# A longer hand-written order of exponentials, projections and V products in the first attention block of a transformer layer

## The chip, the cores and the metric

The kernel runs on one core of one Trainium2 chip. The metric is device time in microseconds (us), the median of the timed runs. A core has five engines that run their own instruction streams and wait for each other through semaphores: PE (TensorE, matrix products), ACT (ScalarE, here the exponentials), DVE (VectorE), POOL (GpSimd) and SP (which issues DMAs here).

## What is computed

A pre-norm transformer layer for 2048 tokens of width 512: attention with 32 query heads of width 16 that share one key head and one value head, then a gated feed-forward network of width 1792, both with a residual.

```python
h  = x + softmax(heads(ln(x) @ wq) @ (ln(x) @ wk).T * 16 ** -0.5) @ (ln(x) @ wv) @ wo
h2 = h + (gelu(ln(h) @ w_gate) * (ln(h) @ w_up)) @ w_down
```

All inputs are float32. Most products are made of split operands, a high and a low part, in three terms.

## The kernel before, in words

**Blocks, groups, exponentials.** The 2048 queries are four blocks of 512. A block has eight groups of four heads (`NG`), and a group has 16 chunks of 128 keys (`KC`). One chunk of one group is a *pair* of exponentials. One exponential is one tile `s` of 128 keys x 2 heads x 512 queries: two score matmuls on PE (L460, `s<-qg,kaug`) into PSUM, then one ACT instruction (L464, `p<-s`) that reads the tile and writes half of a tile `p`. So a group has 32 exponentials and a block 256. They are counted by `n`; group k of the first block holds n = 32(k-1) to 32k-1. In the first block there are three tiles `s` (two of one pool, one more while `width` is 1) and five tiles `p` (`PB`).

**V products.** When both exponentials of a pair are done, the pair can be multiplied with V: function `weigh` (L468, `acc<-p,v_sb`), four matmuls side by side in column strips of 32, which the profile shows as 8 records. This is called a *run*. The 16 runs of a group add up in one PSUM bank, `acc`, of which there is one. After run 15 `evacuate` copies the bank to SBUF on DVE (L481, `oT<-acc`), and its result goes through a DRAM buffer (`acc_d`, `oc`) to be divided by the softmax sums (reciprocals, L509, and two or three more DVE steps), in small steps that are taken out of a list, `outs`, one per run. Run 0 of the next group writes the same bank. Pairs that wait for their run stand in the list `pend`; `finish(n)` does the n oldest.

**The projection beside it.** In the first block PE also projects the queries of blocks 2 to 4 (`project_q`, L458, `pq<-xT,wq`): 12 blocks of work of two halves, each half 12 half-height matmuls ("tokens"), 288 tokens in all. A half-height product uses 64 of the 128 rows of PE, a score uses 50, so that a product and a score run side by side. An exponential of kind "m" (mixed) takes two tokens with it; one of kind "s" takes none. When a half ends inside a step, the rest of that step's "m" are done as "s". After each half DVE makes a mark (L243), after each block a copy (L258), then a split into high and low (L143, L144) and squares (`qs`), which feed a norm on PE (L294, `pqn`). While a norm is due, a step is done without products.

**The order.** A loop (`while n < lead`) writes out the first block. Each turn is a *step*: a word of kinds such as "mms", then a number of runs. PE, ACT, POOL, and in this block DVE and SP too, execute in just that order. Before the change the step is found by `r % 10`, with r = n mod 32: `MIXED = {0: ("mms", 2), 3: ("smm", 1), 6: ("mm", 1), 8: ("ss", 1)}`, and for r of 30 and 31 "sm" or "mm" with one run. The word is made lighter or heavier by comparing the tokens that are left with the exponentials up to `LAST_Q` = 258. A step does its runs only if more than two pairs wait. At 7 places of a group, a further piece of the splitting of the weights is put on POOL (`parts`, for w_gate, w_up, w_down and wo), which loads, splits and stores for the later blocks.

Behind the first block the other work (the feed-forward network of the block before) is woven between the exponentials by another loop.

Of the kernel before, what the change touches and what calls it, by code (L numbers as in the profile page):

```python
# [39 lines left out]
LAST_Q = 258  # L40
# [15 lines left out]
EARLY_PARTS = (8, 11, 16, 21, 26)  # L56

MIXED = {0: ("mms", 2), 3: ("smm", 1), 6: ("mm", 1), 8: ("ss", 1)}

RUNS = ((0, 1, 2, 3), (4, 5, 6, 7), (8, 9, 10, 11), (12, 13))  # L60

# [14 lines left out]
def kernel(  # L76
# [26 lines left out]
    KC = S // P  # L103
# [70 lines left out]
    def attend(first):  # L174
        with ExitStack() as outer:
            with tc.manual_schedule(
                engines={mybir.EngineType.PE, mybir.EngineType.Pool, mybir.EngineType.Activation}
            ):
                run(outer, first)


    def run(outer, first):
# [10 lines left out]
        def psum1(name):  # L193
            return ps.tile([P, T], F32, tag="d", bufs=width, name=name)
# [172 lines left out]
        def later_q():  # L367

            for b in range(1, NB):
                yield from project_q(b, range(DC), nc.vector, b, ())  # L370
            yield REST
            yield REST
            norms.pop()()

        def age():
            for entry in after:
                entry[0] -= 1
            while after and after[0][0] <= 0:
                after.pop(0)[1]()
# [95 lines left out]
        def take_out():  # L475
            for step in outs.pop(0):
                step()
# [202 lines left out]
        def load_wo(b):  # L680

            for j in range(DC // 2):
                w = ring_tile(f"wo_{b}_{j}")
                nc.sync.dma_start(
                    w.bitcast(F32),
                    wo_d[2 * j : 2 * j + 2].rearrange("c p i d -> p c i d").bitcast(F32),
                )
                wos[b, 2 * j], wos[b, 2 * j + 1] = w[:, 0], w[:, 1]
# [680 lines left out]
        PER = NG * KC  # L1369
# [5 lines left out]
        def finish(n):  # L1375
            for _ in range(min(n, len(pend))):
                pb, pg, pkc, pp, pacc, _ = pend.pop(0)
                weigh(pacc, pp, pkc)
                if pkc == KC - 1:
                    evacuate(pb, pg, pacc)  # L1380
# [17 lines left out]
        def score(n, beside=()):  # L1398

            nonlocal acc  # L1400
            i, u = divmod(n, 2)
            b, r = divmod(i, PER)
            g, kc = divmod(r, KC)
            if u == 0:
                if kc == 0:
                    cur["qg"] = qgs.pop((b, g))
                    acc = pss.tile([P, T], F32, tag="acc", bufs=1, name=f"acc_{b}_{g}")
                if kc == 2 and b * NG + g + 1 < NB * NG:
                    key = divmod(b * NG + g + 1, NG)
                    qgs[key] = load_q(*key)  # L1410
                cur["p"] = sb.tile([P, 4, T], F32, tag="p", bufs=PB, name=f"p_{i}")
            scores(i, cur["p"], cur["qg"], kc, u, beside)
            if u == 1:
                pend.append((b, g, kc, cur["p"], acc, n))
# [12 lines left out]
        n, lead = 0, 2 * PER + sum(SIZES[: LEAD[0]])  # L1427
        with tc.manual_schedule(engines={mybir.EngineType.SP, mybir.EngineType.DVE}):
            parts = None
            if first:  # L1430
                work = later_q()
                parts = part_weights(early.enter_context(tc.tile_pool(name="parts", bufs=1)))

            token, left, wo_due = None, 6 * (NB - 1) * DC * DC, True
            while n < lead:
                age()
                r = n % (2 * KC) if n >= 2 * KC else n - START if n < 28 else 30
                if first and n == START:
                    token = next(work)
                if (token is None or token == REST and left <= 0) and (n < START or n % 2 == 0):  # L1440
                    kinds, runs = "ss", 1
                elif r < 30:
                    kinds, runs = MIXED[r % 10]
                    if kinds == "ss" and 10 * left > 13 * (LAST_Q - n):
                        kinds = "sm"
                    elif kinds == "mm" and 10 * left < 11 * (LAST_Q - n):
                        kinds = "sm"
                else:
                    kinds, runs = ("mm" if 10 * left > 13 * (LAST_Q - n) else "sm"), 1
                rest, held = token == REST, False  # L1450
                if wo_due and (n >= LOAD_WO or not first):
                    load_wo(0)
                    wo_due = False
                if n == 2 * PER + CLOSE:
                    assert token is None
                    while after:
                        age()
                    for _ in parts or ():
                        pass
                    if first:  # L1460
                        check_bound(eb, k2m)
                    while outs:
                        take_out()
                    parts = work = None
                    early.close()
                    db = late.enter_context(tc.tile_pool(name="dense", bufs=1))
                    primed = dense(0)
                    next(primed)
                for kind in kinds:
                    if kind == "m" and not rest and not held and token not in (None, REST):  # L1470
                        held = token[1] == 1
                        tokens = token, next(work)
                        score(n, [(lane, step) for lane, _, step in tokens])
                        token = next(work, None)
                        left -= 2
                    else:
                        score(n)
                    n += 1
                    if first and n in TURN_V:
                        turn_last(TURN_V[n])  # L1480
                    if first and n in BUSY:
                        bank = psum1(f"busy_{n}")
                        for _ in range(3):
                            nc.tensor.matmul(
                                bank, kaug[:KR, :P], cur["qg"][:KR, 0, :],
                                start=True, stop=True,
                            )
                if first and n == 4:
                    for _ in q_rest:
                        pass  # L1490
                if rest:
                    token = next(work, None)
                if len(pend) > 2:
                    finish(runs)
                while squares:
                    squares.pop(0)()
                for _ in range(runs):
                    if outs and not pause[0] and n % (2 * KC) not in (2, 3, 4):
                        take_out()
                    pause[0] = max(pause[0] - 1, 0)  # L1500
                if parts is not None and (
                    n in EARLY_PARTS or n > 2 * KC - 4 and n % (2 * KC) % 10 in (0, 6)
                ):
                    next(parts, None)
            assert n == lead
# [14 lines left out]
        kinds = (  # L1520
            ["long"] * 4 + ["gap"] + ["woven"] * 6 * len(SIZES) + ["long"] * 4 + ["short"] * 2
        )
# [332 lines left out]
    def check_bound(sb, k2m):  # L1855
        q2m = sb.tile([H, 1], F32, name="q2m")
        nc.vector.tensor_reduce(q2m, q2, axis=AX.X, op=ALU.max)
        nc.vector.tensor_tensor(q2m, q2m, k2m, op=ALU.mult)
        nc.sync.dma_start(b_d.rearrange("o h -> h o"), q2m)
# [79 lines left out]
```

## Time and profile before

| | |
|---|---|
| median of 3 runs | 1402.85 us (1401.99 to 1403.02) |
| the profiled execution | 1402.12 us, of which the span of its instructions is 1400.0 us |
| granted TensorE clock, mean | 0.998 |
| first exponential of group 1 / 2 / of block 2 | 50.0 / 81.1 / 293.3 us from the start of the span |
| groups 2 to 8 together | 212.24 us |
| PE busy / ACT busy over the span | 99% / 77% |
| V products (L468) | 4096 records, mean 598 ns |
| exponentials (L464) | 1024, mean 1029 ns |

How to read it: the page gives each engine's busy time; a group of instructions is named by its line, engine and the tiles it writes and reads (`out<-in`). A matmul's record is longer than its share of PE, since matmuls overlap; the chain of waits (the work that ended last, followed back) gives the time that each really took on the way to the end. A window gives the busy times of one stretch.

### The profile page before, as it was taken

The numbers are of one execution on the slowest core, as the hardware profiler recorded it, in microseconds if no ns is written. First come the engines' busy times: TensorE is split into PE (matmuls) and PEld (weight loads), VectorE is DVE, ScalarE is ACT, GpSimd is POOL, SyncE is SP. The second block draws the span as 40 slices with busy tenths as digits, with TensorE's granted clock in tenths as the row PEclk, the third lists the DMA queues.
The fourth block names the chain that finished last, engine by engine and source line by source line (L and its number), as shares of the span: only waits on it lengthen the run. The fifth ranks groups of instructions, "written<-read, shape, count | busy, mean of one in ns | idle before, by whom it ended". The sixth has DMA issues, their size and how long they took to land.

```text
span 1400.0 us, 27081 instructions
## 1 busy us (share of the span) xinstructions
PE 1384.4 (99%) x10868; PEld 787.4 (56%) x10868; DVE 558.7 (40%) x1028; ACT 1080.5 (77%) x1246; POOL 531.6 (38%) x975
## 2 busy tenths in 40 slices
PE   8999999999999999999999999999999999999998
PEld 7533333335555555555555555554555555557997
DVE  7322323323353533333253442513343242427666
ACT  7799999997777887777787777877787777775443
POOL 6688877102675660001666651000665500003000
PEclk9999999999999999999999999999999999999999
DMA  4588788533553543134474553224455440334982
GB/s 161 166 248 262 245 271 259 178 106 109 181 206 115 182 160 105 56 112 148 141 227 133 174 171 99 73 88 136 146 195 170 137 145 32 138 125 166 358 294 102
DMA packets 82774, 228.17 MB, mean 163 GB/s; under 512 B 13928, under 2 KB 13928, under 8 KB 82608
## 3 DMA queue, kind: packets, MB, share of 16 engines
q1 hardware_dynamic: 61448, 160.46, 35.0%
q0 software_dynamic: 20448, 64.75, 13.8%
q8 instruction: 87, 1.43, 0.4%
q10 hardware_dynamic: 744, 1.15, 0.2%
q14 instruction: 47, 0.39, 0.1%
HBM read 158.67 MB, written 67.37 MB: 161 GB/s over the span
## 4 chain that ended last, share of the span: by engine, by line
PE 94%; ACT 3%; DVE 1%; issue 1%; DMA 1%; POOL 0%; SPq 0%; POOLq 0%; ACTq 0%; DVEq 0%
PE acc L468 34%; PE s L460 19%; PE pg L1080 8%; PE pu L1080 8%; PE pd L1080 5%; PE pq L458 4%; PE pd L710 3%; PE pd L1202 3%; ACT p L464 3%; PE pa L1272 2%; PE pp L710 2%; PE pb L1272 1%; PE pp L875 1%; PE pc L1272 1%; PE pxt L810 1%
## 5 line engine op out<-in xcount | busy, mean ns | idle before, releaser
L464 ACT ACTIVATE p<-s 128x1024 f32<-128x1024 f32 x1024 | 969.6, 1029 | 223.0 <-PE s L460 218.5
L468 PE MATMUL acc<-p,v_sb 128*32 128x512 f32 x4096 | 494.7, 598 | 0.0
L460 PE MATMUL s<-qg,kaug 50*128 50x512 f32 x1984 | 415.4, 423 | 3.8 <-ACT p L464 3.7
L460 PEld LDWEIGHTS s<-qg,kaug 50*128 50x128 f32 x1984 | 194.1, 184 | 218.4 <-ACT p L464 120.3
L468 PEld LDWEIGHTS acc<-p,v_sb 128*32 128x32 f32 x4096 | 109.8, 109 | 228.2 <-issue 225.3
L1080 PE MATMUL pu<-x2h,w 64*128 64x512 f32 x672 | 211.9, 391 | 0.0
L1080 PE MATMUL pg<-x2h,w 64*128 64x512 f32 x672 | 211.1, 391 | 0.0
L1080 PEld LDWEIGHTS pu<-x2h,w 64*128 64x128 f32 x672 | 116.0, 185 | 14.3
L1080 PEld LDWEIGHTS pg<-x2h,w 64*128 64x128 f32 x672 | 116.0, 185 | 14.0
L1080 PE MATMUL pu<-x2l,w 64*128 64x512 f32 x336 | 122.1, 391 | 0.0
L1080 PE MATMUL pg<-x2l,w 64*128 64x512 f32 x336 | 122.1, 391 | 0.0
L153 POOL TENSOR_SCALAR rstd<-mv 128x1 f32<-128x1 f32 x16 | 3.6, 222 | 298.0 <-DVE mv L151 297.9
L634 POOL DMA_DIRECT2D ws_d<-sp x168 | 95.9, 571 | 51.7 <-POOL sp L144 49.6
L1080 PE MATMUL pd<-w,gh 64*128 64x512 f32 x384 | 81.2, 392 | 0.0
L1022 DVE TENSOR_TENSOR h<-h,pd 128x512 f32<-128x512 f32 x48 | 31.9, 686 | 119.7 <-PE pd L1080 70.6
L1556 DVE SCALAR_TENSOR_TENSOR ga<-ga,g 128x512 f32<-128x512 f32 x70 | 50.0, 715 | 56.4 <-ACT ga L957 55.4
L481 DVE COPY oT<-acc 128x512 f32<-128x512 f32 x32 | 22.1, 692 | 112.0 <-PE acc L468 112.0
L144 POOL TENSOR_TENSOR xlp<-xp,xhp 128x512 fp32r<-128x512 f32 x4 | 5.1, 1288 | 153.8 <-ACT xhp L141 153.8
L1080 PEld LDWEIGHTS pg<-x2l,w 64*128 64x128 f32 x336 | 58.0, 185 | 7.2
L1080 PEld LDWEIGHTS pu<-x2l,w 64*128 64x128 f32 x336 | 58.0, 185 | 6.9
L144 POOL TENSOR_TENSOR sp<-st,sp 128x128 fp32r<-128x128 f32 x120 | 57.9, 483 | 9.7
L509 DVE RECIPROCAL oc<-oc 128x128 f32<-128x128 f32 x64 | 55.6, 916 | 10.2 <-DMA oc<-acc_d 5.2
(326 smaller groups left out, 1892.4 us busy)
## 6 DMA issues: line engine op xcount, KB each, us to landing
w<-w_d SPq DMA_DIRECT2D x88, 512.0 KB
w<-w_d SPq DMA_DIRECT2D x28, 1024.0 KB
ws_d<-sp POOLq DMA_DIRECT2D x168, 128.0 KB, 2.3
ws<-ws_d SPq DMA_DIRECT2D x42, 512.0 KB
wo<-wo_d SPq DMA_DIRECT2D x8, 1024.0 KB
acc_d<-oT SPq DMA_DIRECT2D x31, 256.0 KB
oc<-acc_d SPq DMA_DIRECT2D x124, 64.0 KB
w_d<-w_0b POOLq DMA_DIRECT2D x14, 512.0 KB, 5.8
```

The source lines that it names most:

```text
L144: (eng_lo or nc.vector).tensor_tensor(lo, src, hi.bitcast(F32), op=ALU.subtract)
L458: step()
L460: nc.tensor.matmul(s[:, a, :], kaug[rows, kc * P : (kc + 1) * P], qg[rows, 2 * u + a, :], start=True, stop=True,)
L464: nc.scalar.activation(p[:, 2 * u : 2 * u + 2, :], s, AF.Exp, scale=SCALE)
L468: nc.tensor.matmul(acc[32 * j : 32 * j + 32, :], v_sb[:, kc, :], p[:, j, :], start=(kc == 0), stop=(kc == KC - 1), skip_group_check=True,)
L509: nc.vector.reciprocal(oc[:, 1, sl], oc[:, 1, sl])
L634: nc.gpsimd.dma_start(ws_d[n, j, :, k, c].bitcast(F32), part.bitcast(F32))
L710: nc.tensor.matmul(banks[k], lhsT[rows], rhs[rows], start=(turn == 0 and i == 0), stop=(turn == 1 and i == n - 1), skip_group_check=True,)
L1080: nc.tensor.matmul(e["bank"], lhsT[rows], rhs[rows], start=i == 0 and not e["both"], stop=last and e["both"], skip_group_check=True,)
L1202: nc.tensor.matmul(bank, lhsT, rhs, start=(i == 0), stop=(i == len(terms) - 1))
L1272: nc.tensor.matmul(view[:, k, :], lhsT, rhs, start=fresh and k == 0 and i == 0, stop=i == len(terms) - 1, skip_group_check=True,)
L1556: (soon or lazy).pop(0)()
```

## The change

Groups 2 to 8 (n from 32 to 255) get a table of their own, `LONG_MIX`, of 13 steps over all 32 exponentials of a group, in place of the ten that `MIXED` repeats. Twelve of the steps have runs, four of them two; the last has none. Its words too are made lighter or heavier by the tokens that are left, by other thresholds. The places of the weight parts are moved to ends of the new steps (`PART_AT`), seven in a group as before.

```diff
 MIXED = {0: ("mms", 2), 3: ("smm", 1), 6: ("mm", 1), 8: ("ss", 1)}
+
+LONG_MIX = (
+    ("s", 1), ("mm", 1), ("mms", 2), ("smm", 1), ("mms", 2), ("sms", 1), ("mm", 1), ("mmm", 1),
+    ("sm", 1), ("mms", 1), ("ss", 2), ("sss", 2), ("sm", 0),
+)
+PART_AT = (0, 6, 9, 15, 20, 25, 30)
...
             token, left, wo_due = None, 6 * (NB - 1) * DC * DC, True
+            long_mix, at = {}, 0
+            for kinds, runs in LONG_MIX:
+                long_mix[at] = kinds, runs
+                at += len(kinds)
             while n < lead:
...
                 if (token is None or token == REST and left <= 0) and (n < START or n % 2 == 0):
                     kinds, runs = "ss", 1
+                elif r in long_mix and 2 * KC <= n < 2 * PER:
+                    kinds, runs = long_mix[r]
+                    if kinds in ("ss", "sss", "sms") and 100 * left > 106 * (LAST_Q - n):
+                        kinds = kinds[:-1] + "m"
+                    elif kinds == "mmm" and 100 * left < 98 * (LAST_Q - n):
+                        kinds = "mms"
                 elif r < 30:
                     kinds, runs = MIXED[r % 10]
...
                 if parts is not None and (
-                    n in EARLY_PARTS or n > 2 * KC - 4 and n % (2 * KC) % 10 in (0, 6)
+                    n in EARLY_PARTS
+                    or 2 * KC - 4 < n <= 2 * KC and n % (2 * KC) % 10 in (0, 6)
+                    or 2 * KC < n and n % (2 * KC) in PART_AT
                 ):
                     next(parts, None)
```

## The prediction, made before the changed kernel was run

> **What bounds the kernel now.** I read the page first: its span, its engines, and the chain of waits by engine.
>
> ```profile
> span 1400.0 us, 27081 instructions
> PE 1384.4 (99%) x10868; PEld 787.4 (56%) x10868; DVE 558.7 (40%) x1028; ACT 1080.5 (77%) x1246; POOL 531.6 (38%) x975
> PE 94%; ACT 3%; DVE 1%; issue 1%; DMA 1%; POOL 0%; SPq 0%; POOLq 0%; ACTq 0%; DVEq 0%
> ```
>
> PE sets the end. But 99% is an average over the whole kernel, so I next cut out the stretch that the change touches: one window per group, from the first exponential of groups 2, 3 ... 8 to that of the next.
>
> ```profile
> core 0: us, PE busy (x) PEld busy (x) DVE busy (x) ACT busy (x) POOL busy (x), PEclk, DMA share, GB/s
> 81.10:111.17 30.07, 30.07 (x234) 11.41 (x230) 4.40 (x7) 29.80 (x33) 24.18 (x34) 1.00 0.82 253
> 111.17:141.25 30.08, 30.05 (x232) 11.40 (x228) 8.89 (x10) 29.77 (x33) 24.93 (x33) 1.00 0.88 268
> 141.25:171.65 30.40, 30.39 (x232) 11.43 (x228) 12.09 (x16) 29.90 (x34) 23.66 (x32) 1.00 0.81 247
> 171.65:201.75 30.10, 30.08 (x232) 11.32 (x228) 6.18 (x10) 29.74 (x33) 23.98 (x30) 1.00 0.84 260
> 201.75:231.82 30.07, 30.05 (x232) 11.26 (x228) 11.53 (x14) 29.74 (x33) 23.39 (x31) 1.00 0.82 263
> 231.82:262.75 30.93, 30.93 (x238) 11.97 (x236) 6.94 (x12) 29.91 (x34) 16.39 (x23) 1.00 0.67 210
> 262.75:293.34 30.59, 30.59 (x238) 11.80 (x234) 8.63 (x15) 29.89 (x33) 0.00 (x0) 1.00 0.41 130
> 81.10:293.34 212.24, 212.15 (x1614) 80.60 (x1610) 58.65 (x84) 208.75 (x225) 136.53 (x178) 1.00 0.75 233
> ```
>
> Here PE and ACT are both full: a plain group of 32 exponentials takes 30.07 us. Groups 4 and 7 (30.40, 30.93) hold a norm of the projection, group 8 (30.59) three more projection pairs. Which of the two is late is told by the chain inside one group (the sixth), and by an undisturbed row of exponentials in the same group:
>
> ```profile
> by line: PE acc L468 48.8%; PE pq L458 30.6%; PE s L460 24.0%; issue 0.2%
> ...
> 202.36 1.85 PE acc L468 x16
> 204.21 0.43 PE s L460 x2
> 204.64 0.23 PE pq L458
> 204.87 0.23 PE s L460
> ...
> 205.57 1.00 PE acc L468 x8
> 206.57 0.42 PE pq L458
> ...
> 208.46 0.65 PE s L460 x4
> 209.11 1.00 PE acc L468 x8
> ```
>
> ```profile
> 204.69 8.36 ACT L464 ACTIVATE p<-s 128x1024 f32<-128x1024 f32 x9
> ```
>
> ```profile
> L464 ACT ACTIVATE p<-s 128x1024 f32<-128x1024 f32 x1024 | 969.6, 1029 | 223.0 <-PE s L460 218.5
> ```
>
> The chain runs through PE alone. ACT by itself needs (8.36 - 1.03) / 8 = 0.916 us per exponential, 29.3 us per group, so a plain group loses 0.8 us to PE. All that the change can win on ACT is 212.2 - 7 x 29.3 = 7.1 us.
>
> **The prices.** On the chain a phase of V products costs 1.00 us with one run (8 matmul records) and 1.85 with two (16). The first score slot behind a phase costs 0.43, each later slot 0.23; an exponential without projection ("s") is one slot, one with it ("m") two. So a phase saved by joining two of them is worth 1.00 + 1.00 - 1.85 + 0.43 - 0.23 = 0.35 us. Seven groups before: 70 phases of one run, 21 of two, 224 + 129 slots: 108.9 + 39.1 + 60.3 = 208.3, with some 1.6 for the two norms 209.9 of the 212.2; the rest is waiting.
>
> **What the change does to the order.** I followed the loop by hand through both orders. Before, a group enters with two pairs waiting, and its first steps give the runs 14 and 15 of the old group, then, after three scores, run 0 of the new one. The new order ends a group without a run, enters with three pairs waiting, and gives 13, then 14, then **15 and 0 in one phase** (the step "mms" with two runs at exponential 3); then 1; 2 and 3; 4; 5; 6; 7; 8; 9 and 10; 11 and 12. It does so in each of groups 2 to 8 (group 2 itself enters with two pairs and skips the first run). There are 55 phases of one run and 28 of two (one run fewer, since run 13 of the last group slips out), and 224 + 128 slots: 55.0 + 51.8 + 35.7 + 61.9 = 204.4, or 206.0 with the norms. That is 3.9 us less PE work, 0.85 of it only moved.
>
> **The added wait.** Run 15 closes a group's sum, which DVE copies from the single acc bank (L481); run 0 of the next group writes that same bank. Before, a step of scores stood between. Rows on the copy, in groups 6 and 3, and all that PE ever waited for it in the seven groups:
>
> ```profile
> 202.29 1.92 PE L468 MATMUL acc<-p,v_sb 128*32 128x512 f32 x16
> 204.14 0.50 PE L460 MATMUL s<-qg,kaug 50*128 50x512 f32 x2
> ```
>
> ```profile
> 204.28 0.69 DVE L481 COPY oT<-acc 128x512 f32<-128x512 f32 x1 [4.88 <-PE acc L468]
> ```
>
> ```profile
> 113.71 0.69 DVE L481 COPY oT<-acc 128x512 f32<-128x512 f32 x1 [9.82 <-PE acc L468]
> ```
>
> ```profile
> 114.70 1.07 PE L468 MATMUL acc<-p,v_sb 128*32 128x512 f32 x8
> ```
>
> ```profile
> PEld acc L468 <- DVE oT L481: 0.7, 2, 0.4
> ```
>
> The V phase ends at 202.29 + 1.92 = 204.21, the copy starts 0.07 later and takes 0.69. The hand-over back to PE is not seen under load: it is at most the 0.30 from 114.40 to 114.70, and I bound it below by the 0.07 of the other direction. So the joined phase costs 1.00 + 0.07 + 0.69 + (0.07 to 0.30) + 1.00 = 2.83 to 3.06 in place of 1.85: 0.98 to 1.21 more, I take 1.1. Behind the waiting run 0 on PE stand the scores of the next three exponentials, and ACT waits for these.
>
> TensorE: Matmul & The Clock Gate (Part 2, the LDWEIGHTS step) of the Trainium skill says that PE pulls weight loads ahead but keeps matmuls in program order. No row here shows a score that overtook a waiting V product; if one could, the wait would be filled and the first rival below would hold.
>
> **What ACT can bridge.** There are three score buffers. When PE issues the last score of a step, ACT has at best three exponentials before it, 2.57 us (3 x 0.916, less 0.11 by which an exponential's 1.03 overlaps the next, and a hand-over taken as 0.07). A phase of two runs gives the next score 0.24 + 1.85 later, and ACT starts 0.55 after that score (204.14 to 204.69): 2.64, with the 0.1 to 0.2 that a just released score adds a stall of 0.2. A phase of one run leaves about 0.65 in hand. With 1.1 more the joined phase cannot be bridged at all.
>
> The ledger of a plain group (step price on PE less ACT's need): s +0.31, mm +0.29, mms with two runs and the copy +0.45 + 1.1, smm -0.40, mms with two +0.45, smm -0.40, mm +0.29, mmm -0.17, sm +0.06, mms with one -0.40, ss with two +0.68, sss with two 0.0, sm without a run -0.94. Starting at 0.65 in hand behind run 13: after mm 0.36, then the joined phase falls 1.19 short; the phase of 2 and 3 0.05 short; that of 9 and 10 0.06 short; the last step refills. Stalls of 1.3, so 30.6 us: +0.55 on 30.07. The ledger knows no order inside a step: a phase followed by "m" gives its exponential one slot (0.23) later, which happens at up to two places, and the hand-over may be 0.30: +0.55 to +1.3. I take the middle, +0.95: seven groups **+6.65**.
>
> Smaller terms. In groups 2 to 4 the projection is behind the new pace, and "ss" and "sss" become "sm" and "ssm" right at the two joined phases, where nothing is in hand: two slots, 0.46 x 3 = **+1.4**. The norms now fall in groups 4 and 6, both behind a phase of two runs:
>
> ```profile
> 239.23 0.75 PE pqn L294 x3
> 239.98 1.07 PE acc L468 x6
> ```
>
> The norm and one run take 1.82 in place of 1.00; twice 0.85 is 1.7, against the 0.31 + 0.85 + 0.51 that groups 4, 7 and 8 exceeded 30.08 by before: **0.0**. The run that slips out is done behind the block, where four runs stand on the chain already:
>
> ```profile
> 313.15 3.57 PE acc L468 x32
> ```
>
> **+0.85**, or nothing if ACT covers it. The weight parts of POOL still come seven times a group, at most one exponential earlier: nothing, since POOL has a fifth of each group free and is done before group 8 (0.00 in its window); without that cover a late part would delay the weights' stores, not PE. On SP the turn-out of acc_d is now issued right behind its write and waits there; the queries' writes behind it are needed a group later or more: nothing. Five p tiles: four waiting and one being written use all five, but the run that frees the next was issued a step before: nothing.
>
> Sum: 6.65 + 1.4 + 0.0 + 0.85 = +8.9. The profiled execution took 1402.12 us (2.12 around its span), so 1411.0; it lay 0.73 below the median of 1402.85, on whose scale it is **1411.8**.
>
> **Rivals.** One, faster: the copy costs nothing, because the two runs do not meet or the wait is bridged. For it: fewer phases are plainly cheaper, 0.35 each, and in two groups before PE met the copy for 0.7 us in all without a longer group (30.08 for group 3). Against: there three scores lay between, now none. It gives -3.9 + 0.85 = -3.0, so 1399.8, and at the very best ACT's floor, 1395.7. TensorEngine Tiling (Key Properties) of the Trainium skill, by which a change of tiling mode drains PE, speaks for it: by that rule alone, fewer changes of mode are a gain. It decides if the copy wait is under about 0.4 us a group.
>
> Two, no change: the wait is there, but PE, having 3.9 us less to do, makes up for it: +7.7 - 3.9 + 0.85 = +4.6 if no buffer ever blocks PE in between, and within 2.8 us of before only if the last steps of a group, where PE runs ahead by 0.94, are saved up for it. Against: three buffers cap that at 0.65. The same time comes out if the new table is not reached at all; but the exponential numbers of its steps fit (32 per group), so hardly.
>
> Three, slower still: the copy queues on DVE behind the splitting of a projected block, where one ends in step "mm" (groups 3 and 8):
>
> ```profile
> L1496 DVE TENSOR_TENSOR qs<-qh 128x512 bf16<-128x512 f32 x10 | 11.4, 1137 | 0.0
> ...
> L144 DVE TENSOR_TENSOR ql<-pq_raw,qh 128x512 fp32r<-128x512 f32 x10 | 8.1, 806 | 0.3
> L258 DVE COPY pq_raw<-pq 128x512 f32<-128x512 f32 x10 | 6.9, 692 | 56.9 <-PE s L460 42.4 <-PE pq L458 14.5
> L143 DVE CAST qh<-pq_raw 128x512 fp32r<-128x512 f32 x10 | 6.6, 664 | 0.3
> ```
>
> These make 0.69 + 0.66 + 0.81 + 1.14 = 3.3 us, and by the chain's prices run 15 ends some 3.5 us after the block does: just free. If DVE's slower instances met it (3 us late in both groups) it would be 1417.8.
>
> **How the numbers follow.** The forecast 0.82, rival one 0.06, rival two 0.08, rival three 0.04. The low end takes +0.55 a group and nothing else (1406.7, given as 1406.5, next to rival two's +4.6); the high end takes +1.3 a group with the smaller terms (+11.4, 1414.3, given as 1415). Outside lie rivals one and three and most of two. About 0.2%, 2.8 us, is what a measurement of this kernel can tell from no change: faster 0.06, same 0.08, slower 0.86.
>
> **What would show it.** Right: PE waits for DVE's oT seven times, near 1 us each; the chain passes once a group through the copy (0.69) between two V phases of one run; groups of about 31 us, and ACT idle once in each for more than a microsecond. Wrong: groups under 30.1 us, no DVE on the chain, or a row of 16 V matmuls across the boundary of two groups without a gap; a delay that appears behind 293 us in place of inside the groups would mean that the slipped run or the dense start, not the copy, costs the time.

## The result and the profile after

The changed kernel takes 1414.33 us (median of 6 runs, 1413.91 to 1414.64) against 1402.65 for the kernel before, measured beside it: a ratio of 1.0083 (95% interval 1.0070 to 1.0096), slower by 11.7 us. The lines between the new table and the loop are six higher now: the score is L466, the exponential L470, the V product L474, the copy L487.

The page of the changed kernel: span, engines, and the chain by engine.

```profile
span 1412.8 us, 27076 instructions
...
PE 1388.5 (98%) x10868; PEld 788.7 (56%) x10868; DVE 557.1 (39%) x1028; ACT 1080.5 (76%) x1246; POOL 530.5 (38%) x975
...
PE 90%; ACT 4%; DVE 2%; DMA 1%; issue 1%; POOL 1%; SPq 0%; POOLq 0%; ACTq 0%; DVEq 0%
```

As many matmuls and exponentials as before; PE's share of the chain has gone from 94 to 90%. The same windows as before, one per group, 2 to 8, then all seven, then the 32 exponentials behind them (columns: length of the window, then busy time of PE, PEld, DVE, ACT, POOL):

```profile
80.89:112.64 31.75, 30.94 (x236) 12.07 (x234) 3.42 (x7) 29.81 (x33) 27.20 (x38) 1.00 0.81 266
112.64:144.42 31.78, 30.84 (x232) 11.73 (x230) 10.90 (x13) 29.82 (x33) 24.94 (x33) 1.00 0.84 267
144.42:177.05 32.63, 31.40 (x234) 12.13 (x232) 9.28 (x16) 29.85 (x34) 26.02 (x34) 1.00 0.73 229
177.05:208.33 31.28, 30.47 (x232) 11.78 (x230) 8.18 (x11) 29.75 (x33) 23.79 (x31) 1.00 0.84 272
208.33:240.48 32.15, 31.16 (x234) 12.07 (x234) 13.49 (x17) 29.79 (x34) 21.41 (x30) 1.00 0.73 213
240.48:271.94 31.46, 30.32 (x226) 11.35 (x226) 4.94 (x8) 29.75 (x33) 13.58 (x17) 1.00 0.78 253
271.94:303.24 31.30, 30.30 (x224) 11.60 (x220) 7.01 (x13) 29.78 (x34) 0.00 (x0) 1.00 0.22 59
80.89:303.24 222.35, 215.43 (x1606) 82.72 (x1602) 57.23 (x84) 208.55 (x226) 136.94 (x178) 1.00 0.71 223
303.24:342.82 39.58, 38.13 (x298) 17.13 (x300) 15.86 (x29) 30.33 (x33) 4.41 (x10) 1.00 0.43 133
```

The stretch went from 212.24 to 222.35 us, +10.1. PE, which before was busy for all of it but 0.1 us, now idles for 6.9. The window behind it is 1.35 us longer (39.58 for 38.23). The rest of the kernel repeats itself: the last exponential stands 11.5 us later than before. (The two profiled spans differ by 1.2 us more than that, all of it behind the last DVE instruction, while the output is written.)

The chain at the start of group 6, and ACT there (start, length, what):

```profile
211.17 0.23 PE pq L464
211.41 0.34 PE s L466
211.75 1.04 PE acc L474 x8
212.79 0.02 issue
212.81 0.70 DVE oT L487
213.51 0.04 issue
213.56 1.07 PE acc L474 x8
214.62 0.45 PE s L466 x2
...
215.16 0.66 ACT p L470
...
216.08 1.95 ACT p L470 x2
218.02 0.04 issue
218.07 0.51 PE s L466 x2
```

```profile
209.24 4.71 ACT L470 ACTIVATE p<-s 128x1024 f32<-128x1024 f32 x5
215.16 4.69 ACT L470 ACTIVATE p<-s 128x1024 f32<-128x1024 f32 x5 [1.21 <-PE s L466]
```

Read downwards: run 15, then the copy on DVE, then run 0, then the score for which ACT has been waiting for 1.21 us; then the chain stays on ACT until a score buffer is freed at 218.02. Before, no DVE stood on the chain in these groups:

```profile
by line: PE acc L468 51.3%; PE pq L458 25.9%; PE s L460 22.1%; PE pqn L294 0.7%; issue 0.0%
```

The waits of the changed kernel in the stretch (total, times, longest) say the same:

```profile
PEld acc L474 <- DVE oT L487: 12.0, 7, 1.7
PE acc L474 <- DVE oT L487: 5.7, 7, 0.8
```

Seven times, once a group; before it was 0.7 us, twice.

### The profile page after: what moved, and what is told of

It is laid out like the page before. It is cut to its first block, busy times and chain, and to the rows that moved or that the text cites. A ratio compares the mean times of both kernels' runs of the same rounds, so it can differ in the third digit from the quotient of the medians.

```text
span 1412.8 us, 27076 instructions
## 1 busy us (share of the span) xinstructions
PE 1388.5 (98%) x10868; PEld 788.7 (56%) x10868; DVE 557.1 (39%) x1028; ACT 1080.5 (76%) x1246; POOL 530.5 (38%) x975
## 4 chain that ended last, share of the span: by engine, by line
PE 90%; ACT 4%; DVE 2%; DMA 1%; issue 1%; POOL 1%; SPq 0%; POOLq 0%; ACTq 0%; DVEq 0%
PE acc L474 32%; PE s L466 19%; PE pu L1086 9%; PE pg L1086 8%; PE pd L1086 5%; ACT p L470 4%; PE pq L464 3%; PE pd L716 3%; PE pd L1208 3%; PE pa L1278 2%; PE pp L716 2%; PE pb L1278 1%; PE pp L881 1%; PE pc L1278 1%; DMA x<-in_A_x_dram 0%
## 5 line engine op out<-in xcount | busy, mean ns | idle before, releaser
L470 ACT ACTIVATE p<-s 128x1024 f32<-128x1024 f32 x1024 | 969.6, 1030 | 234.6 <-PE s L466 230.2
L474 PE MATMUL acc<-p,v_sb 128*32 128x512 f32 x4096 | 494.5, 598 | 5.7 <-DVE oT L487 5.7
L466 PE MATMUL s<-qg,kaug 50*128 50x512 f32 x1984 | 417.9, 425 | 5.0 <-ACT p L470 4.4
L466 PEld LDWEIGHTS s<-qg,kaug 50*128 50x128 f32 x1984 | 194.2, 184 | 222.7 <-ACT p L470 124.0
L474 PEld LDWEIGHTS acc<-p,v_sb 128*32 128x32 f32 x4096 | 110.0, 109 | 236.5 <-issue 222.3
L487 DVE COPY oT<-acc 128x512 f32<-128x512 f32 x32 | 22.1, 692 | 99.8 <-PE acc L474 99.6
```

The costliest lines, as they stand in the source:

```text
L466: nc.tensor.matmul(s[:, a, :], kaug[rows, kc * P : (kc + 1) * P], qg[rows, 2 * u + a, :], start=True, stop=True,)
L470: nc.scalar.activation(p[:, 2 * u : 2 * u + 2, :], s, AF.Exp, scale=SCALE)
L474: nc.tensor.matmul(acc[32 * j : 32 * j + 32, :], v_sb[:, kc, :], p[:, j, :], start=(kc == 0), stop=(kc == KC - 1), skip_group_check=True,)
```

## The experiments

Theory A: the wait of run 0 for the copy of run 15's bank is the main cost. Rival B: the order costs by itself, with its four phases of two runs and the projection beside them, and the copy is bridged. The first rival of the prediction also stands to be tested: without the wait, fewer phases would win.

**Nobody reads the bank.**

```diff
-            nc.vector.tensor_copy(oT, acc)
+            if b == 0 and g < NG - 1:
+                nc.vector.tensor_copy(oT, v_sb.rearrange("p k e -> p (k e)"))
+            else:
+                nc.vector.tensor_copy(oT, acc)
```

> The changed kernel, but for the seven groups that close inside groups 2 to 8 of the first block oT is copied from V and not from acc, so that nothing reads the bank and run 0 has nothing to wait for; the order is untouched. Left out: the sums of groups 1 to 7 of the first block never reach the output. Theory A (the wait for the copy is the main cost): each joined phase falls from 2.87 to 1.85 us on the chain, so about 7.3 us come back, groups of some 30.3 us (31 in groups 2 to 4), time near 1407. Rival B (the new order costs by itself, through its four phases of two runs and the projection pairs beside them; the copy is bridged anyway): at most 2 us come back, 1412 or more. First rival of the prediction (without the wait fewer phases win): at or under 1400.

1408.32 us, 6.0 under the changed kernel: about half of the loss, and still 5.8 us above the kernel before, measured beside it (1402.48). In the traces the stretch is 217.29 us, 5.06 less. Not all of the expected 7.3 came back, and the chain of this run shows why:

```profile
208.48 0.34 PE s L466 x2
208.82 1.04 PE acc L474 x8
209.86 0.04 issue
209.91 1.06 PE acc L474 x8
210.97 0.45 PE s L466 x2
```

```profile
PEld acc L474 <- PE acc L474: 7.0, 7, 1.0
```

Run 0 now waits for the end of run 15 itself, seven times. From the first V product to the next score it is 2.15 us (208.82 to 210.97), against 2.87 (211.75 to 214.62) with the copy and 1.85 for an ordinary phase of two. So the joined phase costs 1.02 us more than an ordinary one: 0.72 for the copy (x 7 = 5.04, the 5.06 measured) and 0.30 for the wait that is left when nobody reads the bank. Theory A holds for the larger part of the joined phase. The first rival does not: with the copy gone, the new order is still slower than the old.

**The copy done twice, in both kernels.**

```diff
+            if b == 0 and g < NG - 1:
+                nc.vector.tensor_copy(oT, acc)
             nc.vector.tensor_copy(oT, acc)
```

> The changed kernel with the copy from acc to oT done twice in groups 1 to 7 of the first block. Theory A: PE waits for it to its end, so each of seven boundaries costs 0.69 us more, +4.8 us, about 1419.2. Rival B (copy bridged or only partly on the path): under +2 us.

> The kernel before with the same doubled copy. There run 0 starts 0.53 us behind the end of the copy in five groups and 0.29 in two, so if the copy costs by its place beside run 0, only 0.69 - 0.5 or 0.69 - 0.25 is exposed: +1.5 to +2 us, near 1404.3. If a copy costs its full length wherever it stands (DVE as the limit): +4.8 us, as in the changed kernel.

1419.57 us in the changed kernel: +5.2, and +5.7 us in the traces' stretch (228.09), 0.82 for each of seven copies. In the kernel before 1403.77 against 1402.48, +1.3 (stretch 214.33, +2.1). By the stretches (5.7 and 2.1) the same work costs 2.7 times as much where run 0 stands right behind run 15. Rival B's "bridged" is out.

**Three scores between 15 and 0.**

```diff
-    ("s", 1), ("mm", 1), ("mms", 2), ("smm", 1), ("mms", 2), ("sms", 1), ("mm", 1), ("mmm", 1),
+    ("s", 1), ("mm", 1), ("mms", 1), ("smm", 2), ("mms", 2), ("sms", 1), ("mm", 1), ("mmm", 1),
```

> The changed kernel with the two runs of the third step moved by one: the third step does run 15 alone, the fourth does runs 0 and 1, so three scores lie between 15 and 0; twelve phases and four phases of two as before. Theory A: the wait is bridged, about 5.6 us come back, near 1408.7 (more projection lies beside the phase of 0 and 1, so less than in the run without a reader). Rival B: the time stays within 2 us of the changed kernel. First rival of the prediction: under 1402.

1408.17 us, as expected by theory A, and in the trace no V product waits for oT. Moving one run by one step gives back 6.2 us. But 5.7 remain over the kernel before, with no wait for the bank left. That is the part of the order itself, the slipped run included, and rival B has that much right.

**The runs meet in the old order.**

```diff
+                if 2 * KC <= n < 2 * PER and r in (0, 3):
+                    runs = {0: 1, 3: 2}[r]
                 rest, held = token == REST, False
```

> The kernel before, but in groups 2 to 8 the step at 0 does one run (14) and the step at 3 does two (15 and 0), so that the copy meets run 0 in the old order; thirteen phases, three of two runs, as before. Theory A: 1.0 us of wait in each of seven groups and a worse place for a phase of two, one stall of 1.8 to 1.9 us where 0.2 was: groups of 31.7 us, 1414 to 1415. Rival (the wait costs only in the new order): within 2 us of before.

1413.50 us, 0.5 below the expected range, and the wait as in the changed kernel:

```profile
PEld acc L468 <- DVE oT L481: 12.1, 7, 1.7
PE acc L468 <- DVE oT L481: 5.7, 7, 0.8
```

The old table, thirteen phases, and the weight parts where they were: making 15 and 0 meet is enough to lose 10.8 us. Not all of this is the wait, which by the 1.02 us of a joined phase is 7.1. The rest would be the worse place of a phase of two that the expectation names: in group 5 ACT idles 1.71 us at it, against 1.20 in the changed kernel. No run has this place without the wait.

**Twelve phases without a meeting, in the old order.** In the run without a reader some 3 us of the stretch are still open (217.29 - 7 x 0.30 - 212.24 = 2.95). About 1.4 of them is the heavier projection in groups 2 to 4 (there group 2 takes 31.03 us and group 5 30.59); the other 1.5 is 0.22 in each group. This run asks what a fourth phase of two costs when the rest of the order stays.

```diff
+                if 2 * KC <= n < 2 * PER and r in (28, 30):
+                    runs = {28: 0, 30: 2}[r]
                 rest, held = token == REST, False
```

> The kernel before, but in groups 2 to 8 the step at 28 does no run and the step at 30 does two: runs 12 and 13 in one phase, twelve phases a group as in the change, and no phase holds both 15 and 0. Theory (ACT is left alone): the fourth phase of two runs stalls ACT by 0.55 to 0.65 us, 1406.4. Rival (the prediction's price of a phase, PE as the only limit): 0.35 us less in each group, 1400.0.

1406.68 us, +3.9 or 0.56 a group: the theory's number, and the prediction's price of a phase has the wrong sign here. ACT at the end of group 6 in this run:

```profile
227.02 7.43 ACT L464 ACTIVATE p<-s 128x1024 f32<-128x1024 f32 x8
235.11 1.03 ACT L464 ACTIVATE p<-s 128x1024 f32<-128x1024 f32 x1 [0.65 <-PE s L460]
```

And in the kernel before, around the same place (the end of group 6 is at 231.82 there), one row without an idle gap:

```profile
223.49 12.33 ACT L464 ACTIVATE p<-s 128x1024 f32<-128x1024 f32 x13
```

The chain of the same run shows what PE did before that gap:

```profile
230.65 1.07 ACT p L464
231.72 0.04 issue
231.76 0.49 PE s L460
...
232.26 0.23 PE s L460
232.49 1.85 PE acc L468 x16
234.34 0.42 PE pq L458
```

PE has to wait for a score buffer, which ACT frees at 231.72. From then on ACT has three exponentials, until 234.45 (2.73 us). PE does the slots that are left of its step and the phase of two, and the next exponential starts at 235.11, 3.39 us behind the release. So PE saves a phase and ACT stands still for 0.65 us: in this place the phase of two is longer than three score buffers can bridge. No run had another number of buffers.

**The projection pairs moved.**

```diff
-                    if kinds in ("ss", "sss", "sms") and 100 * left > 106 * (LAST_Q - n):
-                        kinds = kinds[:-1] + "m"
+                    if r in (12, 20, 22) and 100 * left > 106 * (LAST_Q - n):
+                        kinds = {12: "smm", 20: "mm", 22: "mmm"}[r]
```

> The changed kernel, but when the projection is behind, the pairs are added in the steps at 20 and 22 (sm to mm, mms to mmm) in place of those at 25 and 27, which stand beside the two joined phases 9, 10 and 11, 12. As many pairs in the block, as many phases. Theory (a slot costs its 0.23 us only where ACT has nothing in hand): groups 2 to 4 come down from 31.75, 31.78 and 32.63 by 0.3 us each, the time by about 1.1, to 1413.2. Rival (PE is the limit and a slot costs the same anywhere): 1414.3, groups 2 to 4 as in the changed kernel.

1413.08 us, within the noise of the expected 1413.2; the groups tell it better (2, 3, 4):

```profile
80.88:112.26 31.38, 30.57 (x234) 11.90 (x232) 3.43 (x7) 29.78 (x34) 25.98 (x37) 1.00 0.80 266
112.26:143.75 31.49, 30.54 (x234) 12.02 (x234) 10.24 (x13) 29.77 (x33) 23.35 (x30) 1.00 0.81 257
143.75:175.96 32.21, 30.98 (x234) 12.19 (x234) 9.71 (x16) 29.79 (x34) 28.46 (x38) 1.00 0.79 252
```

They lose 0.37, 0.29 and 0.42 us, 1.1 in all. The same slot costs less beside a phase of one run.

**The slipped run.**

```diff
                     elif kinds == "mmm" and 100 * left < 98 * (LAST_Q - n):
                         kinds = "mms"
+                    elif kinds == "sm" and n == 2 * PER - 2:
+                        runs = 1
```

> The changed kernel, but the last step of group 8 has one run, so that run 13 no longer slips out of the block behind it. The run costs some 1.0 us behind the block (the traces differ by 1.05 us between exponentials 272 and 288) and, beside the last step of group 8, which is behind nothing, some 0.3 us. Expected 0.7 us under the changed kernel, 1413.6. Rival (the slipped run costs nothing of its own): 1414.3 or more.

1412.86 us, 1.5 under the changed kernel, more than expected. In the traces the 32 exponentials behind the stretch come back to 38.45 us from 39.58, and group 8 takes 0.34 more; the last exponential is 0.7 earlier, as expected. The slip cost about that; the remaining 0.8 of the difference of the medians has no place that the traces show.

**Another table in the same place.**

```diff
-    ("s", 1), ("mm", 1), ("mms", 2), ("smm", 1), ("mms", 2), ("sms", 1), ("mm", 1), ("mmm", 1),
-    ("sm", 1), ("mms", 1), ("ss", 2), ("sss", 2), ("sm", 0),
+    ("mss", 2), ("smm", 1), ("ms", 1), ("ms", 1), ("mmm", 1), ("mm", 1), ("sm", 1), ("mms", 2),
+    ("sss", 2), ("smm", 1), ("sm", 1), ("ms", 1), ("mm", 1),
 )
-PART_AT = (0, 6, 9, 15, 20, 25, 30)
+PART_AT = (0, 6, 10, 15, 20, 26, 30)
...
-                    if kinds in ("ss", "sss", "sms") and 100 * left > 106 * (LAST_Q - n):
+                    if kinds in ("ss", "sss", "sms") and 100 * left > 120 * (LAST_Q - n):
...
-                    elif kinds == "mmm" and 100 * left < 98 * (LAST_Q - n):
+                    elif kinds == "mmm" and 100 * left < 95 * (LAST_Q - n):
```

> Another table in the same place: mss 2, smm 1, ms 1, ms 1, mmm 1, mm 1, sm 1, mms 2, sss 2, smm 1, sm 1, ms 1, mm 1, with thresholds 120 and 95. Thirteen phases, three of two runs, two of which follow each other (the second behind three scores without projection), runs 15 and 0 three scores apart, no run slips out. Theory (what counts is how long ACT is left alone beside a phase of two runs, not the number of phases): the stall of the third phase of two runs goes, about 0.15 us a group, so 1401.5, 1.0 us under the kernel before. Rival (a phase saved is worth 0.35 us, so twelve phases are needed for a gain): 1402.5 or more.

1401.94 us against 1402.75, a ratio of 0.9995 (0.9986 to 1.0004): not told apart from the kernel before. The trace has the stretch 0.5 us shorter, with PE busy throughout:

```profile
81.06:292.79 211.73, 211.73 (x1612) 82.47 (x1612) 54.68 (x83) 207.69 (x225) 135.14 (x178) 1.00 0.74 234
```

A long table is no loss in itself, but this one won nothing that can be measured.

## Why the prediction was right, point by point

**The added wait** was the mechanism, with the predicted size: 2.87 us for the joined phase (2.83 to 3.06), with 0.06 for the hand-over from DVE (213.50 to 213.56), about the low bound. The scores behind it on PE did wait, as the Trainium skill has it (TensorE: Matmul & The Clock Gate, Part 2): none overtook run 0 in the chain. The run without a reader splits the 1.02 us: not all is the copy.

**The plain group** was mis-sized. Groups 5 and 8 take 31.28 and 31.30 us where a plain group took 30.07: +1.2, within the ends of 0.55 to 1.3 but above the 0.95 chosen, so the term of 6.65 should have been 8.5. The ledger alone gave 0.55, and the range held by the allowance on top of it. Neither reason for that allowance shows: the hand-over came at its low bound, and in the new table an "s" follows every phase of two, while no phase of one costs group 5 more than 0.08. That the size fell within the range is in part luck. ACT in group 5 of the changed kernel:

```profile
183.86 5.61 ACT L470 ACTIVATE p<-s 128x1024 f32<-128x1024 f32 x6 [1.20 <-PE s L466]
189.67 19.70 ACT L470 ACTIVATE p<-s 128x1024 f32<-128x1024 f32 x21 [0.20 <-PE s L466]
```

The ledger had the joined phase fall 1.19 short, and ACT idles 1.20 there. Where an exponential's row does not overlap the one before it by the usual 0.11, more than the idle time is lost, so I also take the starts of the exponentials in this trace, less 0.916 each. The joined phase then loses 1.38 us, the phase of 2 and 3 0.35, that of 9 and 10 0.29, that of 11 and 12 0.07. What the ledger missed are these others: it gave 0.05, 0.06 and nothing, by letting PE carry time in hand from step to step; the joined runs 12 and 13 in the old order show PE held at a score buffer instead. In the kernel before, the three phases of two of this group lose 0.24, 0.32 and 0.23, though its rows show no idle gap. Without a reader the joined phase loses 0.67: the 0.30 of the wait that is left, and 0.37 like an ordinary phase of two.

**The smaller terms** held. Projection in groups 2 to 4: 0.47 and 0.50 above group 5, and 32.63 - 31.28 - 0.87 = 0.48 in group 4 (0.87 being the norm, by group 6): 1.45 for 1.4. Norms: 2 x 0.87 for 1.7. The slipped run: 0.7 for 0.85. Together 8.5 + 1.45 + 0.1 + 0.7 = 10.7 of the 11.5 us by which the last exponential is late; group 7 (31.46, one more heavy step at 27) has 0.2 of the rest, and 0.6 is left without a place. So the sum of 8.9 was low, and the result lies only 0.7 under the high end of the range.

**The saving** of 3.9 us of PE work was worked out from prices, and it bought nothing. In group 5 of the changed kernel a phase still costs 1.00 or 1.85, the joined one aside. But the 51 slots take 14.95 us by their starts, where the prices give 14.1; before, 50 slots took 14.60, also for 14.1. Several of the late slots stand just ahead of a phase of two (0.42 and 0.43 us where 0.32 is usual), and the weight loads of the scores wait for ACT 76 times in the stretch, with or without a reader of the bank, where they waited 64 times before. That PE spent the saved time waiting for score buffers is my reading of this; PE's busy time can't show it, since it went up (212.15 to 215.43). So the first rival fell (1408.3 without the copy and 1408.2 without any wait, not 1399.8), and with it, for these orders, the bare rule that fewer changes of tiling mode are a gain. The second rival's +4.6, PE's sum with the wait, fell by the same reason. The third did not come up: in group 3 the squares ended on DVE just as run 15 did, and the copy began at once.

## What to carry to other kernels

When work is joined into longer phases on a shared engine, count not the phases but how long the other full engine is left alone beside each, against what its buffers hold. When an accumulator has one bank, the last product of one sum and the first of the next must not stand side by side: keep as much other work between them as the copy and its hand-overs take (here 0.8 us). Follow a hand-written order across the boundary of its repetition, where the state that it enters with (pairs waiting) decides which work meets.

## What the runs showed that I had not expected

A sum that begins in the bank of the one just ended waits for it on PE even when no other engine reads the bank: 0.30 us in each of seven groups, put down to `acc` itself (7.0 us of weight-load waits). The profile infers such a wait from a semaphore, here one that PE sets itself at the end of run 15, so it is a wait that the program asks for. Whether the result needs it, and whether a second bank would remove it, was not tried.

The doubled copy cost 0.82 us apiece on the path, more than the 0.69 of its record. In the trace 0.03 of this lies between the two copies, and run 0 starts 0.15 behind the second copy, where it started 0.05 behind the only one; why is open.
